# Another written-out order of all instructions on the five engines of an attention and MLP kernel

## The chip, the cores and the metric

The program runs on one core of one Trainium2 chip. A core has five engines with a queue each: TensorE (PE, matrix products; its weight loads are shown apart as PEld), VectorE (DVE), ScalarE (ACT), GpSimd (POOL) and SyncE (SP, which here issues every DMA). An engine works its queue strictly in order; between engines an instruction waits on semaphores. The metric is device time in microseconds of one execution, less is better. The kernel before took 799.24 us in the median of 3 runs (798.97 to 799.45).

## The reference

Three stages, all in float32, on 4 batches x 576 positions = 2304 tokens:

```
scores = scale * q @ k^T, causal;  a = softmax(scores);  local = a @ v
mem_out = (phi(q) @ M_prev) / (phi(q) . z_prev + 1e-6);  phi(x) = elu(x) + 1
x  = g * mem_out + (1 - g) * local          g = sigmoid(beta), one per head   8 heads x 64
x1 = (s * relu(x @ w_in)^2 + b) @ w_out     512 -> 2048 -> 512
h  = x1 @ w2_in                             512 -> 1024
y  = layernorm(h * softmax(h)) * g_ln @ w2_out      1024 -> 512
```

## The kernel before

Matrix products of the two MLPs split each float32 operand into a high and a low part and add three products (high x high, high x low, low x high), so every product is three `128x512` or `128x256` matmuls per 128 rows of depth. The larger ones are done by a Strassen-like scheme on 2x2 blocks: the block products are named X, Y, V and W.

The program has three stretches, by the trace:

- Attention, 0 to about 260 us. Sixteen pairs of heads, u = 0 to 15. For each pair: scores `s` (L730, L761), a row minimum by DVE into `mx` and the exponential by ACT (L713), transposes `pp` of the probabilities on PE (L787, and L799 for the last chunk into `ppu`), their copies `pt` by ACT (L791) and `ptl` by DVE (L800), then the values `po` (L819) and `pe` (L831), and the memory term (L835, L837) whose operand `mq` POOL weighs (L685) and DVE makes (L678). Beside it runs the first quarter of the first MLP as filler (`first_part`, `hidden`: L850 to L852, L913 to L915), and ACT and DVE decode and split the weights (`fetch`, `split_w`: L485 to L514).
- The rest of the first MLP, to about 600 us (`second_part`): ten rounds, each one block of tokens and six of the twelve remaining slices f of the hidden width. `y2_r_c` is the result of round r in output chunk c, `X_r_f` to `W_r_f` are the block products. Between PE steps stand the leaving operations: ACT copies (L1134, L1159), DVE additions (L1150 to L1166), the activation on ACT (L1126 to L1129) and its low part on DVE (L1130), and the addition of `y2` to `yT` on DVE (L1185). POOL builds the next round's block sums (L979 to L987) and the weights' sums (L530, L540).
- The second MLP, to the end (`mlp2`): nine pairs of token tiles; products a to d (L1273 to L1276), softmax and norm (`front`), transposes `zt` (L1322), copies `zh` (ACT, L1325) and `zl` (DVE, L1326), and the output product (L1331 to L1333).

What sets the order: nothing is left to a scheduler. `ORDER` is a table of runs `a+n` for each engine; a number is an instruction's place in the order in which the program text makes it, `a+n` means n of them from a. `state_order` chains each instruction to the one before it in that list, so the queue of each engine is exactly the list. `SLOTS` fixes which buffer each tile gets. The waits follow from the data and from the buffers.

```
for x, y in zip(seq, seq[1:]):
    tc.add_manual_dep(y, x.name, info, reason="order")
```

Of the kernel before, what the change touches and what calls it, by code (L numbers as in the profile page):

```python
# [26 lines left out]
0+22 34+4 22+6 46 38+2 48+8 28+2 47 62 30 66 31+2 63 33 40+3 64+2 43+3 67 56+2 71+2 58 73 59+2 68+3 114+2 74+6 116+4  # L27
84 80 85 81+2 86 83 87 102+4 61 88+4 106+4 92+3 96 95 122+4 110+4 97 101 98+3 147 120+2 126+6 148 132+2 149+2 146
151 195+2 155+6 134+2 161+2 197+2 163+2 136+8 183+2 144+2 185+3 165 152 166 153 167+2 154 203+4 199+2 207+4 169+4
177 188+4 173+3 178 176 179+2 438 181 228 182 192+2 201+2 211+4 236+6 215+2 194 217+10 229+4 439 227 233 242+2 234+2  # L30
244+2 284+2 276+2 286+2 278+4 288+4 246+4 440 250+4 264+4 254+3 258 257 268+8 259 263 260 309 261+2 282+2 308 310
292+16 317+2 357+4 319+4 361+2 441 311+6 345+4 442 323 327+2 324+3 329+2 365+8 331+4 443 390 444+3 335+5 349+8 344
340+4 389 391 363+2 373+4 398+6 377+12 447+3 392+3 430+6 450+8 395+3 408+2 483+5 404 410+2 405+3 488+7 412 418+4
527+5 417 413+4 532+7 436+2 495+6 580+5 475 585+6 476 591 458+12 422+6 470+2 428+2 472+2 539+4 547+2 543+2 549+6
477+2 480+3 479 624+5 505+2 501 507 502+2 508 504 629+2 474 631+2 509 633+3 510+5 572 669+7 573 676 545 555+3 546
558 515+10 592+4 636+2 596+2 677+4 574+3 559+6 525+2 565+4 644+2 638+2 646+2 640+2 648+4 569+2 721 577+3 598+4 722+3
602+5 725 571 611 607+4 726 681 727+6 682 642+2 652+4 689+2 733+4 691+2 737+2 693+2 612+10 656+8 622+2 664+2 766+3
683+3 666+2 769 668 770 695 686+2 696 688 697+2 741+8 771+2 699+5 773+2 778 708 704+4 709+4 749+4 739 775+3 779+4
740 786+4 818+2 790+2 713+4 753+2 717+2 755+6 719+2 761+2 838+6 820+2 844+2 822+2 783+3 826+5 792+4 765 831 796+4
832 763+2 806+6 833 805 800 834+4 863 846 801 847+3 802+3 886+12 865+2 824 867 825 864 923+12 850+8 812+2 858+2  # L40
814+2 860+2 816+2 915+2 871+6 968+2 881+3 868 884 869+2 970+10 877+4 917+2 935+2 919+2 937+6 885 1020+7 902 898+3
1027+3 960 1030+2 862 901 943+4 1065+11 961 1076 921+2 903+4 980+6 907+2 947+10 909+2 957+2 911+4 965+3 962 1109+4
986+4 1113+4 963+2 994 1012+2 1032+2 1014+2 1034+4 1016+2 1038+2 995 990+3 996+2 993 998 1117+2 1057 999 1119 959
1058 1120 1018 1040+4 1019 1077+4 1121+4 1081+2 1000+10 1044+8 1010+2 1052+4 1059+3 1129+4 1125+2 1154 1083 1062
1084 1063+2 1085+2 1155+5 1091 1133+4 1092+4 1087+3 1160+3 1090 1096 1163+4 1056 1239+3 1167 1242 1137+3 1127 1140
1128 1097+6 1174+2 1206+4 1176+2 1210+2 1178+2 1141+10 1103+6 1151+2 1168+3 1243 1153 1244+2 1171+3 1214+8 1180+3
1246 1183 1247+4 1184+3 1189+2 1187 1191+2 1251 1274+2 1188 1276+6 1193 1282+4 1252 1212 1222+2 1213 1224+2 1194+4
1336+12 1259+2 1303+4 1261+4 1226+2 1198+2 1228+6 1200+4 1234+2 1204+2 1236+2 1253+3 1371+4 1256 1265+3 1257 1268
1258 1307+2 1311+8 1375+3 1269 1273 1270+3 1378+3 1286+5 1348 1238 1381 1349 1382 1309+2 1356+4 1400+2 1360+2 1402+4
1291+12 1350 1319 1351 1320 1352 1321+2 1408+4 1362+4 1323+12 1412 1370 1413+2 1353+3 1383+4 1335 1366+4 1415+5 1445  # L50
1387 1420+8 1388+4 1428+2 1406 1430+2 1407 1462+4 1446 1432+8 1392+4 1440+2 1396+2 1442+2 1398+2 1466 1447 1453+4
1448+2 1467+4 1461 1471+3 1450 1474 1451+2 1475+3 1444 1491+12 1457+4 1479+4 1516+3 1478 1519+4 1483+4 1503+8 1487+2
1511+2 1489+2 1513+3 1528 1540+2 1529+5 1523 1534 1542 1535 1543 1536 1544+2 1524 1537 1546+2 1538+2 1548 1525
1549+6 1526 1555 1564 1556 1565+3 1527 1557 1568+3 1558+4 1571+5 1562 1576 1588 1577 1563 1589 1578 1590+2 1579 1592
1580 1593 1636 1624 1637+2 1625+2 1639 1627+3 1640+4 1630 1644 1631 1645 1632 1646 1633 1647 1634+2 1581+3 1594
1584+2 1648+7 1660 1655 1661+3 1656 1664+2 1657 1666 1595+2 1586+2 1597+3 1658+2 1667 1600+3 1612 1603 1613 1604+2
1614 1606+6 1668+4 1615+3 1720 1672+2 1618+6 1674+2 1726 1676+10 1727 1686+2 1721 1688 1696 1689 1697 1690 1698+3
1691+3 1701 1722 1694 1702 1695 1703+5 1728+3 1708 1723 1709+2 1738+4 1711+3 1742 1724 1714 1725 1715+3 1731 1743
1718+2 1744+4 1732+5 1768 1737 1748+2 1769+3 1756+3 1750+6 1759+4 1772 1763+2 1773 1765+2 1774 1780 1775 1781 1776
1767 1782 1777+2 1783+3 1779 1789+5 1795 1794 1786 1796 1804 1787 1813+2 1805 1815 1788 1806 1816+4 1822 1820 1823  # L60
1807 1824+2 1808 1826 1821 1809+4 1840 1797 1858 1798+2 1828 1800 1829+2 1827 1801 1831 1802 1832 1803 1859 1841
1867+3 1833+5 1843+2 1838 1845 1839 1846 1861+3 1847 1864+3 1860 1842 1849 1852 1848 1853+5 1879 1870 1850+2 1876
1871 1873+2 1872 1877 1880 1878 1875 1882 1906+2 1894 1915 1895 1908+2 1916 1900 1917+2 1896 1910 1901+2 1897+2 1911
1903 1899 1904 1919+2 1905 1888 1885 1881 1886 1891 1889 1883+2 1892+2 1890 1924 1948 1966+2 1925+2 1968 1936 1927
1949 1937 1928 1938 1969 1950 1939 1929 1951+3 1940+2 1970+2 1930 1912 1960+6 1978+2 1972 1980 1973 1981 1974+2 1987
1976 1988 1977 1989 1982+2 2020 1990+2 1931 1887 1921 2005+4 1992 2009+2 1933+2 1932 1913 1954 1922 1935 1914 1955
1957 1942 1923 1943 1958 1945+2 1944 1947 1959 1956 1996+2 2014+6 1998+4 2021+2 2026 2023 2027 2024 2028+2 2032+2
2030 2034 2025 2031 2035 2041 2036 2042+2 2037 2044+3 1984+2 2059+2 2050 2061 2051+5 2062+3 1993+2 2002 1995 1986
2011 2047 2012+2 2003 2038+2 2048 2040 2049 2065 2004 2066 2092+2 2104+4 2094 2113 2098 2108 2095 2114+3 2096 2117
2097 2118 2056 2068 2057+2 2067 2099 2109 2100+2 2122+2 2102+2 2124+2 2074 2069 2077 2071 2075 2072 2070 2073 2083  # L70
2076 2084 2080 2086 2081 2078+2 2146+3 2134 2149+2 2126 2135 2127 2151 2136 2164+2 2137+2 2166 2139 2158 2167 2159+4
2170+2 2176 2163 2172+3 2177 2175 2178+2 2168 2180+2 2169 2087 2082 2110 2089+3 2088 2128 2111 2085 2218 2185 2203+3
2186+2 2206 2219+2 2207+2 2188 2221+2 2189+2 2129 2112 2130 2140+2 2194 2212 2195+2 2224 2197+3 2225+2 2213 2227+2
2214 2223 2215 2230+2 2216+2 2229 2232 2119+3 2152 2142 2131 2143 2132+2 2155 2153 2144 2156+2 2145 2154 2239+2 2233
2257 2234 2241+2 2258 2235 2259+2 2243 2261+2 2244 2200 2182 2201+2 2209 2254 2183+2 2191 2236 2302+2 2290 2248 2291
2249 2304 2250+3 2292 2305 2253 2306 2293+3 2307 2192+2 2210 2245 2211 2255 2246 2256 2263+2 2237+2 2265 2247 2311+2
2296+3 2313 2299 2314+2 2300+2 2316 2266 2272 2275 2269+3 2273 2267 2276 2268 2278 2350 2338 2351+3 2339+5 2354+3
2274 2277 2344+5 2357+3 2349 2360+2 2287 2281 2279 2282 2284 2288 2283 2289 2285 2280 2286 2374+6 2308+2 2323 2310
2324 2326 2320 2325 2321 2335+2 2317+2 2337 2322 2332 2327 2319 2328+4 2333+2 2380 2386+6 2381+2 2392+3 2368 2362
2369 2395 2383 2396 2370 2384 2397 2385 2365 2455 2404 2371 2366+2 2405 2401 2363+2 2398 2446+2 2456 2399 2448  # L80
2457+2 2434+3 2402 2400 2372 2449 2403 2437 2406 2438 2373 2459 2407 2416 2410 2440 2411+2 2450 2408 2422 2417 2409
2419 2423 2413 2441+2 2424 2439 2418 2443 2428 2460 2444+2 2420 2451 2464+2 2452 2414+2 2466 2429 2467+2 2488 2469
2425 2453 2489 2421 2426 2431 2490 2500 2491+2 2501 2493 2502+2 2427 2506 2461 2504 2476+3 2507 2430 2454 2512
2508+2 2479+3 2505 2462 2470 2463 2432 2513+2 2433 2510 2473 2515 2511 2527 2471 2474 2518 2516 2519 2472 2528 2517
2520 2529 2560+2 2494 2530 2475 2545 2495 2521 2485 2546+2 2522 2496 2548 2523 2549 2531 2482+2 2532 2550 2562+2
2536+3 2484 2539+3 2564 2486 2554+3 2566 2497 2557+2 2487 2567 2498 2565 2568 2559 2569+2 2499 2572 2571 2573+2
2581+2 2575 2533 2524 2534+2 2583 2599 2576 2584 2577 2600+2 2585 2525 2551+2 2542 2553 2543 2586 2602+2 2590+2 2604
# [1317 lines left out]
```

## Time and profile before

| | |
|---|---|
| median of 3 runs | 799.24 us (798.97 to 799.45) |
| the profiled execution, as timed | 797.52 us |
| its span, first to last instruction | 795.7 us |
| PE busy | 784.8 us (99% of the span), 5298 matmuls |
| DVE, ACT, POOL busy | 598.6 (75%), 567.7 (71%), 155.6 us (20%) |
| granted TensorE clock over the span | 1.00 |
| chain that ended last | PE 82%, DVE 7%, ACT 4%, issue 3%, DMA 2% |

Line numbers as L831 are those of the kernel's text. An idle time in brackets at the end of a timeline row is the time in which the engine did nothing before that instruction, and behind the arrow what ended it. Matmuls overlap in the pipeline: their shown durations are longer than the distance between their starts, so throughput is read from starts.

### The profile page before, as it was taken

Reading aid. Unit: us, or ns where it says so; the run is one execution under the profiler, and the core shown is the slowest. Engines: PE = TensorE matmul, PEld = TensorE weight load, DVE = VectorE, ACT = ScalarE, POOL = GpSimd, SP = SyncE. Lnnn points to the kernel's source line nnn. Section 1 sums busy time; section 2 is a strip of 40 time slices with the busy share of each in tenths; the row PEclk is TensorE's granted clock in tenths of the full one; section 3 lists DMA queues with packets and bytes.
Section 4 is the critical chain, followed back from the end, with each engine's and each line's share of the span. In section 5 each row is a group of like instructions: output and inputs, shape, how many; then the busy total and the mean of one; then the engine's idle time right before and its main releaser. Section 6 shows DMA issues by size and latency. Waiting matters only on the chain.

```text
span 795.7 us, 14760 instructions
## 1 busy us (share of the span) xinstructions
PE 784.8 (99%) x5298; PEld 656.7 (83%) x5298; DVE 598.6 (75%) x1457; ACT 567.7 (71%) x1186; POOL 155.6 (20%) x166
## 2 busy tenths in 40 slices
PE   9999999999999999999999999999999999999998
PEld 7777777877776888889899888889987888888886
DVE  6999988877799888996557778566769665566751
ACT  7999988888897569987868776677746443445542
POOL 3121222122011324140120114000022212121200
PEclk9999999999999999999999999999999999999999
DMA  8463573464847558787687876576563001000001
GB/s 261 148 205 89 168 203 104 153 168 147 290 148 224 198 174 301 253 290 253 215 279 260 288 243 195 191 243 199 188 256 133 1 27 40 14 27 28 26 28 54
DMA packets 63277, 133.47 MB, mean 168 GB/s; under 512 B 9228, under 2 KB 19172, under 8 KB 63204
## 3 DMA queue, kind: packets, MB, share of 16 engines
q1 hardware_dynamic: 63204, 132.53, 50.5%
q8 instruction: 42, 0.69, 0.4%
q14 instruction: 31, 0.25, 0.1%
HBM read 90.97 MB, written 41.53 MB: 167 GB/s over the span
## 4 chain that ended last, share of the span: by engine, by line
PE 82%; DVE 7%; ACT 4%; issue 3%; DMA 2%; POOL 1%; SPq 0%; DVEq 0%; ACTq 0%; POOLq 0%
PE y L1181 5%; PE y L1179 5%; PE y L1180 5%; PE pp L787 5%; PE s L730 5%; PE V L1109 4%; PE X L1109 4%; PE o L1331 4%; PE o L1332 4%; PE o L1333 4%; PE po L819 4%; PE W L1109 3%; PE h L850 2%; PE h L851 2%; PE y L915 2%
## 5 line engine op out<-in xcount | busy, mean ns | idle before, releaser
L1180 PE MATMUL y<-g,w 128*128 128x512 f32 (+1 forms) x240 | 81.2, 370 | 0.0
L1179 PE MATMUL y<-g,w 128*128 128x512 f32 (+1 forms) x240 | 78.7, 371 | 0.9 <-DVE yT L1185 0.9
L1181 PE MATMUL y<-g,w 128*128 128x512 f32 (+1 forms) x240 | 78.9, 370 | 0.0
L713 ACT ACTIVATE pr<-pr,mx 128x128 f32<-128x128 f32 (+3 forms) x128 | 71.0, 558 | 3.8 <-DVE mx L746 3.4
L791 ACT ACTIVATE pt<-pp,omg 128x512 f32<-128x512 f32 (+3 forms) x128 | 62.8, 524 | 10.2 <-PE pp L787 9.1
L746 DVE CUSTOM_DVE_ANT_0 pr<-s,big 128x256 f32<-128x256 f32 (+3 forms) x128 | 59.1, 481 | 10.0 <-PE s L730 8.8
L1109 PE MATMUL X<-fhb,w 128*128 128x256 f32 x240 | 63.4, 285 | 0.7 <-ACT u L1134 0.5
L1109 PE MATMUL V<-fht,w 128*128 128x256 f32 x216 | 57.2, 286 | 0.8 <-ACT yo L917 0.3
L1332 PE MATMUL o<-w,zh 128*128 128x512 f32 x144 | 54.7, 393 | 0.0
L1331 PE MATMUL o<-w,zh 128*128 128x512 f32 x144 | 54.2, 392 | 0.0
L1333 PE MATMUL o<-w,zl 128*128 128x512 f32 x144 | 54.0, 393 | 0.0
L1130 DVE TENSOR_TENSOR g<-r,g 128x512 fp32r<-128x512 f32 (+1 forms) x60 | 40.1, 672 | 17.3 <-ACT r L1129 16.9
L1128 ACT ACTIVATE g<-r,b_sb,s_sb 128x512 fp32r<-128x512 f32 (+1 forms) x60 | 45.6, 767 | 9.7 <-PE y L1181 9.1
L1181 PEld LDWEIGHTS y<-g,w 128*128 128x128 f32 x240 | 44.8, 189 | 6.8 <-DVE g L1130 0.2
L1180 PEld LDWEIGHTS y<-g,w 128*128 128x128 f32 x240 | 44.7, 189 | 6.6
L787 PE MATMUL pp<-ident,pr 128*128 128x128 f32 x320 | 49.4, 276 | 0.2 <-DVE ptl L800 0.2
L1179 PEld LDWEIGHTS y<-g,w 128*128 128x128 f32 x240 | 43.6, 189 | 6.7 <-DVE yT L1185 1.1
L1126 ACT ACTIVATE r<-r 128x512 f32<-128x512 f32 (+1 forms) x60 | 34.7, 582 | 18.4 <-DVE r L1162 8.6
L624 POOL TENSOR_TENSOR q<-ph,zb 128x640 f32<-128x640 f32 x16 | 25.7, 1608 | 111.8 <-DVE ph L621 92.0
L787 PEld LDWEIGHTS pp<-ident,pr 128*128 128x128 f32 x320 | 37.8, 140 | 11.4 <-issue 2.2
L730 PE MATMUL s<-kq 64*128 64x128 f32 x640 | 46.5, 288 | 0.4 <-DVE sm L768 0.3
L1109 PEld LDWEIGHTS X<-fhb,w 128*128 128x128 f32 x240 | 44.3, 190 | 2.9 <-ACT r L1159 0.8
(233 smaller groups left out, 2371.1 us busy)
## 6 DMA issues: line engine op xcount, KB each, us to landing
raw<-in_moe_w_in_dram SPq DMA_DIRECT2D x24, 512.0 KB, 6.5
raw<-in_moe_w_out_dram SPq DMA_DIRECT2D x24, 512.0 KB, 4.1
wd<-wt SPq DMA_DIRECT2D x21, 512.0 KB, 4.7
w<-wd SPq DMA_DIRECT2D x21, 512.0 KB, 7.2
kq<-in_kq_dram SPq DMA_DIRECT2D x16, 608.0 KB, 5.7
RW<-rd SPq DMA_DIRECT2D x24, 288.0 KB, 4.8
q<-in_q_dram SPq DMA_DIRECT2D x16, 320.0 KB, 3.6
v<-in_v_dram SPq DMA_DIRECT2D x16, 320.0 KB, 6.0
```

Of the source, the lines that this page charges most:

```text
L713: mark[0] = nc.scalar.activation(pr, pr, AF.Exp, bias=mx, scale=-1.0, accum_out=sm).ins
L730: self.last = nc.tensor.matmul(ss[:, j, c0 + k * P:c0 + (k + 1) * P], x[:, S + i * P:S + (i + 1) * P], x[:, k * P:(k + 1) * P], start=True ...
L746: nc.vector.tensor_tensor_reduce(pr, ss[:, j, at[i]:at[i] + n], big[:, CF * P - i * P:CF * P - i * P + n], -scale, FMAX, ALU.add, ALU.min, mx)
L787: nc.tensor.transpose(pp[:, e * n + c * P:e * n + (c + 1) * P], pr[:, c * P:(c + 1) * P], ident)
L791: nc.scalar.activation(p["pt", i // 2][:, j, 0:i + 1, i % 2, :], pp[:, e * n:(e + 1) * n].rearrange("p (c t) -> p c t", t=P), AF.Copy, sca ...
L1109: nc.tensor.matmul(o, wc[a], b[:, i, 0:m], start=(i == 0 and z == 0 and not more), stop=(i == KH - 1 and z == 2), skip_group_check=True)
L1179: nc.tensor.matmul(o, wc[0], gh, start=(f == fs[0]), stop=False)
L1180: nc.tensor.matmul(o, wc[1], gh, start=False, stop=False)
L1181: nc.tensor.matmul(o, wc[0], gl, start=False, stop=(f == fs[-1]))
L1331: nc.tensor.matmul(oo, zh, w[:, 0], start=(f == 0), stop=False)
L1332: nc.tensor.matmul(oo, zh, w[:, 1], start=False, stop=False)
L1333: nc.tensor.matmul(oo, zl, w[:, 0], start=False, stop=(f == NF2 - 1))
```

## The change

Only the numbers in `ORDER` change. The instructions, their count on every engine, the buffers in `SLOTS` and all text below are the same; each of the five queues is another permutation of the same list. The new lists come from a search that judged an order by the mean of four replays with drawn lengths and landings. On PE 558 of 4546 instructions keep their place, on ACT 225 of 1005, on DVE 235 of 1243, on POOL 67 of 166, on SP 68 of 366; most move by a few places.

```
 ORDER = {
     "PE": """
-0+22 34+4 22+6 46 38+2 48+8 28+2 47 62 30 66 31+2 63 33 40+3 64+2 43+3 67 56+2 71+2 58 73 59+2 68+3 114+2 74+6 116+4
...
     "SP": """
-17+2 20 32 29 28 21 19 24 27 26 33 25 22 30 23 37 31 41 34 36 42 54 45 39 35 49 40 60 47 44 43 46 38 48 50 53 55 52
+17+2 28 20 19 45 21 23 32 24 33 22 25 46 31 37 41 26 36 30 34+2 39 42 49 40 38 29 54 43+2 47+2 27 50 60 53 55 52
```

Three places, as the built programs list them (operation, output <- inputs, shape; "x2": two alike in a row).

First, DVE at the end of the attention, between the product that closes pair 14 (`po14`) and the copy `ptl` of pair 15's last transposed chunk (`ppu15`), for which the matmuls `pe15` wait. Before:

```order
L838 TENSOR_TENSOR xb3_3005<-po14_3444,RW14_3413 128x512
L678 SCALAR_TENSOR_TENSOR mq15_3481<-kq15_3142,mq15_3481 128x640
L491 TENSOR_TENSOR wa12_2110<-wa12_2110,raw12_2108 128x512
L488 TENSOR_SCALAR raw14_3782<-wa14_3784 128x512
L490 SCALAR_TENSOR_TENSOR raw14_3782<-raw14_3782 128x512
L880 TENSOR_TENSOR xl3_3714<-xb3_3005,xh3_3713 128x320
L509 TENSOR_TENSOR w11_1917<-wa11_1911,w11_1917 128x512
L880 TENSOR_TENSOR xl3_3714<-xb3_3005,xh3_3713 128x320 x2
L491 TENSOR_TENSOR wa14_3784<-wa14_3784,raw14_3782 128x512
L509 TENSOR_TENSOR w13_2260<-wa13_2254,w13_2260 128x512
L800 COPY ptl_137<-ppu15_3619 64x128
```

The same stretch now:

```order
L838 TENSOR_TENSOR xb3_3005<-po14_3444,RW14_3413 128x512
L509 TENSOR_TENSOR w10_1792<-wa10_1786,w10_1792 128x512
L678 SCALAR_TENSOR_TENSOR mq15_3481<-kq15_3142,mq15_3481 128x640
L488 TENSOR_SCALAR raw18_4185<-wa18_4187 128x512
L509 TENSOR_TENSOR w12_2116<-wa12_2110,w12_2116 128x512
L490 SCALAR_TENSOR_TENSOR raw18_4185<-raw18_4185 128x512
L800 COPY ptl_137<-ppu15_3619 64x128
```

Ten instructions stood between the two ends and were passed; now there are five. The three additions L880 stand behind the copy.

Second, DVE in the second round of `second_part` (r = 1), before the addition L1185 that frees the PSUM bank of `y2_0_1`, for which the first matmul of `y2_1_1` waits. Before:

```order
L1150 TENSOR_TENSOR u1_8_4703<-Y_1_8_4698,u1_8_4703 128x256
L1153 TENSOR_TENSOR u1_8_4703<-V_1_8_4699,u1_8_4703 128x256
L1156 TENSOR_TENSOR r2_1_9_4705<-W_1_8_4700,u1_8_4703 128x256
L509 TENSOR_TENSOR wt0_5187<-ss12_5072,wt0_5187 128x512
L1185 TENSOR_TENSOR yT_4102<-y2_0_1_4114,yT_4102 128x512
```

Now:

```order
L1130 TENSOR_TENSOR g2_1_5_4495<-r2_1_5_4498,g2_1_5_4495 128x512
L486 TENSOR_SCALAR wa33_5065<-wa33_5065 128x512
L1156 TENSOR_TENSOR r2_1_7_4619<-W_1_6_4614,u1_6_4617 128x256
L488 TENSOR_SCALAR raw33_5063<-wa33_5065 128x512
L1130 TENSOR_TENSOR g2_1_4_4494<-r2_1_4_4497,g2_1_4_4494 128x512
L1185 TENSOR_TENSOR yT_4102<-y2_0_1_4114,yT_4102 128x512
```

The addition moved ahead of all work on f = 8: in front of it stand results of f = 4 and f = 6, whose products PE has done earlier.

Third, PE in the third round (r = 2), between the last matmul of `X_2_8` and the first of `X_3_4`, which takes over the same PSUM bank once ACT has copied `X_2_8` out (L1159). The last rows before:

```order
L1179 MATMUL y2_2_2_4855<-g2_2_5_4862,w9_1595 128x512
L1180 MATMUL y2_2_0_4853<-g2_2_4_4861,w8_1456 128x512
L1181 MATMUL y2_2_0_4853<-g2_2_4_4861,w8_1456 128x512
L1179 MATMUL y2_2_1_4854<-g2_2_4_4861,w8_1456 128x512
L1179 MATMUL y2_2_0_4853<-g2_2_5_4862,w9_1595 128x512
L1109 MATMUL V_3_4_5226<-fht3_3_5197,w15_3874 128x256
L1109 MATMUL V_3_4_5226<-flt3_3_5198,w15_3874 128x256
L1109 MATMUL X_3_4_5224<-fhb11_3_5191,w14_3804 128x256
```

Now:

```order
L1109 MATMUL X_2_8_5080<-fhb21_2_4816,w22_4241 128x256
L1109 MATMUL V_2_8_5082<-fht4_2_4814,w23_4324 128x256
L1181 MATMUL y2_2_3_4856<-g2_2_4_4861,w8_1456 128x512
L1179 MATMUL y2_2_3_4856<-g2_2_5_4862,w9_1595 128x512
L1180 MATMUL y2_2_3_4856<-g2_2_5_4862,w9_1595 128x512
L1181 MATMUL y2_2_3_4856<-g2_2_5_4862,w9_1595 128x512
L1179 MATMUL y2_2_0_4853<-g2_2_5_4862,w9_1595 128x512
L1109 MATMUL V_3_4_5226<-fht3_3_5197,w15_3874 128x256
L1109 MATMUL X_3_4_5224<-fhb11_3_5191,w14_3804 128x256
```

Between the two stood ten matmuls of `128x512` and two of `128x256` (five of the ten are not shown); now five and two.

## Rows read from the trace of the kernel before

**Rows 1.** The page, busy us of each engine, share of the span, instructions

```profile
PE 784.8 (99%) x5298; PEld 656.7 (83%) x5298; DVE 598.6 (75%) x1457; ACT 567.7 (71%) x1186; POOL 155.6 (20%) x166
```

**Rows 2.** Stretches: from:to, length, then busy us (x instructions) by engine

```profile
0.00:20.00 20.00, 18.85 (x163) 14.44 (x163) 12.83 (x57) 14.43 (x40) 6.92 (x20) 1.00 0.82 262
780.00:800.00 20.00, 12.02 (x53) 9.58 (x52) 1.38 (x2) 2.88 (x5) 0.00 (x0) 0.93 0.15 53
```

**Rows 3.** Waits of PE: instruction <- releaser: us, times, longest

```profile
PE warm L379 <- DVE mhalf L1240: 1.1, 1, 1.1
PE pe L831 <- DVE ptl L800: 1.0, 1, 1.0
PE y L1179 <- DVE yT L1185: 0.9, 1, 0.9
PE zt L1322 <- DVE var L1309: 0.6, 1, 0.6
PE X L1109 <- ACT u L1134: 0.5, 1, 0.5
PE zt L1322 <- DVE sm L1302: 0.4, 1, 0.4
...
```

**Rows 4.** Groups of PE instructions by shape: busy us, mean ns

```profile
L1180 PE MATMUL y<-g,w 128*128 128x512 f32 x192 | 68.7, 392 | 0.0
L850 PE MATMUL h<-xh,w 128*128 128x512 f32 x64 | 27.2, 435 | 0.0
L851 PE MATMUL h<-xl,w 128*128 128x512 f32 x64 | 25.7, 410 | 0.0
```

**Rows 5.** Timeline of PE at 432 us: start, us, instruction, count

```profile
432.41 0.28 PE L1109 MATMUL W<-fht,wh 128*128 128x256 f32 x1
432.53 0.40 PE L1109 MATMUL V<-fht,w 128*128 128x256 f32 x2
...
433.13 0.86 PE L1180 MATMUL y<-g,w 128*128 128x512 f32 x3
433.82 0.40 PE L1181 MATMUL y<-g,w 128*128 128x512 f32 x1
```

**Rows 6.** Timeline from 253 us: DVE, POOL and PE before the copy ptl

```profile
253.01 0.69 DVE L509 TENSOR_TENSOR w<-wa,w 128x512 fp32r<-128x512 f32 x1
...
254.66 1.95 POOL L685 TENSOR_TENSOR mq<-mq,RW 128x640 f32<-128x640 f32 x1 [11.42 <-DVE xl L880]
...
255.12 2.04 DVE L509 TENSOR_TENSOR w<-wa,w 128x512 fp32r<-128x512 f32 x1
...
257.19 0.29 DVE L800 COPY ptl<-ppu 64x128 f32<-64x128 f32 x1
...
257.54 0.69 PE L831 MATMUL pe<-ptl,v 128*64 128x64 f32 x16 [1.03 <-DVE ptl L800]
```

**Rows 7.** Timeline from 342 us: the same engines before y of round 1

```profile
342.84 1.31 POOL L980 TENSOR_TENSOR xr<-xr 128x512 f32<-128x512 f32 x1
...
342.91 1.78 DVE L509 TENSOR_TENSOR wt<-ss,wt 128x512 fp32r<-128x512 f32 x1
...
344.62 1.27 DVE L1185 TENSOR_TENSOR yT<-y,yT 128x512 f32<-128x512 f32 x2
...
345.35 0.50 PE L1179 MATMUL y<-g,w 128*128 128x512 f32 x1 [0.85 <-DVE yT L1185]
```

**Rows 8.** Timeline from 294 us: copies out of PSUM, and PE behind them

```profile
294.12 0.39 ACT L917 ACTIVATE yo<-y 128x256 f32<-128x256 f32 x1 [0.21 <-PE y L915]
...
298.08 0.39 ACT L917 ACTIVATE yo<-y 128x256 f32<-128x256 f32 x1 [0.63 <-DMA yd<-yo]
...
298.52 0.39 PE L1109 MATMUL V<-fht,w 128*128 128x256 f32 x1 [0.28 <-ACT yo L917]
```

**Rows 9.** Timeline from 377 us: the copy by ACT before the first matmul of X_3_4

```profile
378.39 0.36 ACT L1159 ACTIVATE r<-X 128x256 f32<-128x256 f32 x1
...
378.80 0.39 PE L1109 MATMUL X<-fhb,w 128*128 128x256 f32 x1
```

440 rows, old and new, of the table ORDER are left out of this document.

## The prediction

> **What bounds the kernel now.** I read the page first: PE is busy for 784.8 of 795.7 us [rows 1]; no other engine comes near. Then the stretches: the last one shown holds 12.02 us of PE work [rows 2], so the last matmul ends about 3.7 us before the span does, and the final copy and store fill that. What PE idles beyond that stands in its waits. That view has 15 rows of one wait each: 1.1 us before the first matmul, then 1.0, 0.9, 0.6, 0.5 and 0.4, and nine of 0.2 or 0.3 with 2.5 us together [rows 3]. So 5.9 us inside the program are waits on another engine's result, and 5.9 + 1.1 + 3.7 = 10.7 is nearly all of the 10.9 us that PE does not work. An order can win the 5.9, not the start or the end.
>
> There is a second, hidden loss. In the attention the same `128x512` matmul of the filler takes 435 ns (L850) to 410 (L851) where in the later stretch it takes 392 (L1180) [rows 4]. Six lines of 64 matmuls are of this kind, so between 6 x 64 x 18 ns = 6.9 us and 6 x 64 x 43 ns = 16.5 us go there, about 12 in the middle; PE changes between kinds of work there, and a follower starts late.
>
> For cover I need the price of PE work by starts: a `128x256` matmul starts 0.12 us after the one before, a `128x512` one (433.82 - 433.13) / 3 = 0.23 us [rows 5].
>
> **The change part by part.** Nothing is added or removed, so each term is a wait that goes, shrinks or grows. For each I ask how much PE work stands in the order between the last matmul that the awaited result needs (with what is queued ahead of it) and the matmul that waits; call it the cover.
>
> *The copy before `pe15` (1.0 us).* DVE's L509 there took 2.04 us, its neighbour of the same form 0.69 [rows 6]: POOL's L685 ran from 254.66 to 256.61, and L509 ended 0.55 us behind it. The copy (0.29) was queued behind, and PE waited 1.03. Between `po14` and the copy DVE now passes five instructions, not ten; with `po14`'s own addition that is six, at the 0.69 us of an undisturbed L509 each 4.1 us, plus 1.35 if POOL's operation falls on an L509 again: 5.5. PE has 6.9 us of its own work from the end of `po14` to `pe15` (before: 6.4), and about 1.1 us from the chunk's transpose, which the copy with 0.29 us fits into. I take -1.0, ends 0 and -1.0.
>
> *The addition before `y2_1_1` (0.9 us).* Again an L509 beside POOL: 1.78 us, 342.91 to 344.69, with L980 until 344.15; L1185 starts 344.62 and PE idles 0.85 [rows 7]. Now the addition stands ahead of all work on f = 8, with no L509 in the six rows, and its cover grows from 2.25 to 4.5 us. I take -0.9, ends 0 and -0.9.
>
> *The pair of waits at 297 and 298 us (0.5 and 0.3).* The first goes: `X_0_4` now has seven `128x256` matmuls, 0.84 us, behind the last matmul that its copy needs, where it had none, and the copy takes 0.38. What is late next is the second. `yo4_3` takes over the buffer of `yo4_2`, and may be written only when that one's store has landed: copy at 294.12, landed at 298.0, next copy at 298.08, `V_0_4` at 298.52 [rows 8], 4.4 us in all. PE's own work from `y4_2` to `V_0_4` is 3.48 us before and 3.60 now. So the stall of 0.8 moves to V and shrinks by 0.12; I take -0.1, ends 0 and -0.5.
>
> *Six smaller ones.* Before `zt` the cover of the three waits of 0.6, 0.4 and 0.3 grows by 0.23, 1.0 and over 5 us: -0.2, -0.4, -0.3. Three waits of 0.3 (at 234, 411 and 440 us) get 0.7 us of cover or more: -0.9. Together -1.8, ends 0 and -2.2.
>
> *What gets worse.* `X_3_4` waits for ACT's copy L1159 of `X_2_8`. The copy itself is 0.36 us, but ACT came to it only at 378.39, and the matmul started at 378.80 [rows 9]. Cover before: ten and two matmuls, 2.5 us; now five and two, 1.4. If ACT is as late as it was, PE waits 1.1 us more; if ACT is in step, the 0.36 hide and it costs nothing. ACT has nearly the same five operations ahead. Two more places lose 0.5 (`W_0_8` at 316) and 0.4 us (`X_7_10` at 494) of cover. Ends 0 and +2.0; I take the middle, +1.0.
>
> *Changes of kind on PE in the attention.* Counted in the two lists, 373 before and 360 now, 3.5% fewer. Of the hidden 12 us that is -0.4, ends 0 and -0.6.
>
> *Waits not there before.* Over both lists I counted the cover of every wait of PE for ACT, DVE or POOL: 686 and 688. Under 1.0 us there are 57 before and 47 now, under 2.0 us 324 and 294. If waits go with the close ones, 5.9 x 47/57 = 4.9 us would remain, a gain of only 1.0; the named terms give -1.0 - 0.9 - 0.1 - 1.8 + 1.0 - 0.4 = -3.2. The two disagree because a new order has its own unlucky places, which this trace cannot show. I add +0.7 for them, between none and the +2.2 that would bring the two together.
>
> *SP and the weights.* The reloads of weights and block forms keep their distance: the shortest PE work between what releases a reload of a form (L951) and its matmul is 4.1 us before and 5.0 now. At the start the second pair's keys are fifth in SP's list, not eighth. No wait of PE before ends on a landing directly, so I put both at nothing; cover gone there would cost a landing, which was 3.5 us for the store above.
>
> Sum: -3.2 + 0.7 = -2.5 us. On the profiled execution, 797.52 (1.8 around a span of 795.7), that is 795.0. The median of the runs is 1.7 above that execution, so the forecast is 799.24 - 2.5 = **796.7 us**.
>
> **The rivals.** *The waits come back elsewhere (no change).* For it: half the listed gains are single waits of 0.2 to 0.4 us, and 294 places with under 2 us of cover remain, on engines that are 71 and 75% busy [rows 1]. Against it: the close places got fewer in every class. If the whole 3.2 returns, 799.2; with the fewer close ones, 798.2.
>
> *DVE meets POOL at worse places (slower).* The two dearest waits were not of the order alone: each had a DVE addition that took 1.1 to 1.35 us longer beside a POOL operation [rows 6, 7]. DVE's list moved against POOL's nearly unmoved one, so the meetings fall elsewhere. In `second_part`, where POOL builds the block sums of the next round, an L1130 or L509 ahead of an L1153 or L1156 holds up a product on PE. Each such meeting with a cover under 1.2 us costs up to 1.2. It turns slower at four uncovered new ones (4 x 1.2 - 2.5 = +2.3): 801.5 us. For it: W and V products with a cover of 1.1 us are still there. Against: two in 795 us were uncovered before.
> The Trainium skill ("SBUF — State Buffer", section "SBUF: two separate sides") says that VectorE and GpSimd share a port pair as an exclusive lock for a whole instruction, and that a VectorE operation with two SBUF inputs blocks fully against a GpSimd one that reads SBUF. The trace agrees at both places, where the addition ended 0.55 us after POOL's did. By that rule a meeting could cost as much as the whole POOL operation, 1.95 us for L685, and four would give 804.5.
>
> *Everything listed is won and nothing new comes.* All 5.9 us and 0.6 of the changes of kind: 792.7. Little speaks for it, since the store at 298 us stays.
>
> **How the numbers follow.** A measurement of this kernel can tell 0.2%, 1.6 us, from no change; 797.6 and 800.8 are the bounds. The forecast, 794 to 797.6, has 0.52, with 0.05 for the case that all is won below it: faster 0.57. Waits that come back, 797.6 to 800.8, have 0.24; meetings, above 800.8, 0.19. The range leaves out about one in ten on either side: 793.3 to 801.3.
>
> **What would show it.** Right: no row for `pe` L831 and `y` L1179 in PE's waits, or a few tenths; L509 of about 0.7 us ahead of the copy `ptl`; a wait of V for `yo` at about 298 us of 0.6 to 0.9, and none of X there; the waits of PE after the first at 3 to 4 us together; L850 below 435 ns. Wrong: a sum of waits near 5.9, or L1153, L1156 and L1130 stretched above 1 us in front of a waiting W or V; then the slower case holds. If PE's busy time changes by more than 2 us without its waits, my split into waits and changes of kind is at fault.

## The result and the profile after

The changed kernel takes 787.77 us in the median (785.34 to 791.80, six runs) against 799.11 (796.76 to 799.97, six runs) of the kernel before on the same chip: ratio 0.987 (0.984 to 0.990), 11.3 us less. The forecast was 2.5 less, and the time lies below its range. Two later sets of runs gave 786.09 against 797.82 and 786.55 against 797.65.

The page of the profiled execution after (790.62 us as timed, 788.8 span) answers to [rows 1]:

```profile
PE 779.0 (99%) x5298; PEld 657.1 (83%) x5298; DVE 593.4 (75%) x1457; ACT 568.2 (72%) x1186; POOL 155.7 (20%) x166
```

PE works on the same 5298 matmuls and is busy 5.8 us less. The whole list of its waits (instruction, releaser, us, times, longest), against the 15 of [rows 3]:

```profile
PE pp L787 <- ACT pt L791: 2.5, 1, 2.5
PE warm L379 <- DVE mhalf L1240: 1.1, 1, 1.1
PE V L1109 <- ACT yo L917: 1.0, 1, 1.0
PE zt L1322 <- DVE z L1311: 0.7, 2, 0.4
PE pp L787 <- DVE xb L839: 0.4, 1, 0.4
PE s L761 <- DVE mx L746: 0.3, 1, 0.3
```

`pe` and `y` are gone, and X too. The 2.5 and the 1.0 do not come in every execution: a later profile of the same kernel (783.6 us span) has neither. Its page, and its waits after the first matmul's 1.1:

```profile
PE 777.3 (99%) x5298; PEld 655.8 (84%) x5298; DVE 591.9 (76%) x1457; ACT 567.8 (72%) x1186; POOL 155.7 (20%) x166
```

```profile
PE zt L1322 <- DVE z L1311: 0.7, 2, 0.4
PE pp L787 <- DVE xb L839: 0.3, 1, 0.3
PE s L761 <- DVE mx L746: 0.3, 1, 0.3
```

I compare this one with before, since neither is disturbed. The span shrinks by 795.7 - 783.6 = 12.1 us: 7.5 of it is shown as less PE busy time, and only 4.6 as less idle time. To place it, I priced each matmul by the commonest distance from its start to the next, by form (0.227 us for `128x512`, 0.120 for `128x256`, and so on; the same sum for either kernel), and summed what the starts took beyond that. That loss falls from 33.0 to 29.2 us in the attention, from 8.8 to 2.3 in the rest of the first MLP, from 3.1 to 1.5 in the second. Its level depends on how finely forms are told apart, the differences hardly do.

The copy that answers to [rows 6]; timeline of the profile after (start, us, engine, instruction):

```profile
252.96 0.68 DVE L509 TENSOR_TENSOR w<-wa,w 128x512 fp32r<-128x512 f32 x1
...
254.63 0.69 DVE L509 TENSOR_TENSOR w<-wa,w 128x512 fp32r<-128x512 f32 x1
...
256.48 0.29 DVE L800 COPY ptl<-ppu 64x128 f32<-64x128 f32 x1 [0.57 <-PE ppu L799]
...
257.52 0.40 PE L831 MATMUL pe<-ptl,v 128*64 128x64 f32 x8
```

DVE now waits for the transpose, and PE does not wait for the copy. The copies that answer to [rows 8], first in the profile after:

```profile
293.25 0.75 ACT L917 ACTIVATE yo<-y 128x256 f32<-128x256 f32 x2 [1.26 <-PE y L915]
...
297.70 0.38 ACT L917 ACTIVATE yo<-y 128x256 f32<-128x256 f32 x1 [1.23 <-DMA yd<-yo]
...
298.13 0.39 PE L1109 MATMUL V<-fht,w 128*128 128x256 f32 x1 [1.01 <-ACT yo L917]
```

The same copy in the later execution, where the store landed earlier:

```profile
292.40 0.38 ACT L917 ACTIVATE yo<-y 128x256 f32<-128x256 f32 x1
```

### The profile page after: what moved, and what is told of

Same layout as the page of the kernel before. It is cut to its first block, busy times and chain, and to the rows that moved or that the text cites. A ratio compares the mean times of both kernels' runs of the same rounds, so it can differ in the third digit from the quotient of the medians.

```text
span 788.8 us, 14752 instructions
## 1 busy us (share of the span) xinstructions
PE 779.0 (99%) x5298; PEld 657.1 (83%) x5298; DVE 593.4 (75%) x1457; ACT 568.2 (72%) x1186; POOL 155.7 (20%) x166
## 4 chain that ended last, share of the span: by engine, by line
PE 93%; DMA 3%; DVE 2%; issue 1%; SPq 0%; POOL 0%; ACT 0%; ACTq 0%; DVEq 0%
PE y L1179 6%; PE y L1181 6%; PE y L1180 6%; PE pp L787 5%; PE V L1109 5%; PE X L1109 5%; PE s L730 5%; PE po L819 5%; PE W L1109 4%; PE o L1333 4%; PE o L1331 4%; PE o L1332 4%; PE Y L1109 2%; PE y L913 2%; PE zt L1322 2%; PE y L915 2%
## 5 line engine op out<-in xcount | busy, mean ns | idle before, releaser
L1181 PE MATMUL y<-g,w 128*128 128x512 f32 (+1 forms) x240 | 81.3, 370 | 0.0
L1179 PE MATMUL y<-g,w 128*128 128x512 f32 (+1 forms) x240 | 80.2, 370 | 0.0
L1180 PE MATMUL y<-g,w 128*128 128x512 f32 (+1 forms) x240 | 80.1, 370 | 0.0
L713 ACT ACTIVATE pr<-pr,mx 128x256 f32<-128x256 f32 (+3 forms) x128 | 70.9, 556 | 2.0 <-DVE mx L746 1.6
L791 ACT ACTIVATE pt<-pp,omg 128x256 f32<-128x256 f32 (+3 forms) x128 | 62.8, 524 | 11.3 <-PE pp L787 7.4
L746 DVE CUSTOM_DVE_ANT_0 pr<-s,big 128x128 f32<-128x128 f32 (+3 forms) x128 | 58.8, 481 | 10.3 <-PE s L730 9.8
L787 PE MATMUL pp<-ident,pr 128*128 128x128 f32 x320 | 51.6, 278 | 2.9 <-ACT pt L791 2.5
L1332 PE MATMUL o<-w,zh 128*128 128x512 f32 x144 | 54.1, 393 | 0.0
L1331 PE MATMUL o<-w,zh 128*128 128x512 f32 x144 | 52.5, 390 | 0.0
L1325 ACT ACTIVATE zh<-zt 128x512 fp32r<-128x512 f32 x36 | 21.0, 594 | 42.4 <-PE o L1332 29.4
```

Source lines behind the costliest of these rows:

```text
L713: mark[0] = nc.scalar.activation(pr, pr, AF.Exp, bias=mx, scale=-1.0, accum_out=sm).ins
L746: nc.vector.tensor_tensor_reduce(pr, ss[:, j, at[i]:at[i] + n], big[:, CF * P - i * P:CF * P - i * P + n], -scale, FMAX, ALU.add, ALU.min, mx)
L787: nc.tensor.transpose(pp[:, e * n + c * P:e * n + (c + 1) * P], pr[:, c * P:(c + 1) * P], ident)
L791: nc.scalar.activation(p["pt", i // 2][:, j, 0:i + 1, i % 2, :], pp[:, e * n:(e + 1) * n].rearrange("p (c t) -> p c t", t=P), AF.Copy, sca ...
L1179: nc.tensor.matmul(o, wc[0], gh, start=(f == fs[0]), stop=False)
L1180: nc.tensor.matmul(o, wc[1], gh, start=False, stop=False)
```

## The experiments

My theory, formed on the two traces: the gain is waits of PE, and most of a wait is in no row. In the trace before, 49 matmuls start within 0.08 us of the end of the operation that releases them, 28 of them after 261 us; in the trace after it is 13, with 3 after 261 us and 10 in the attention (the expectations of the two halves below have these two the other way round). Those 28 started 6.5 us late together, against the distance of their forms, and the next two starts behind each another 2.6. I call this the start delay. Rivals: only the shown waits count; or the gain is in PE's own order, its changes of kind. Medians stand beside the kernel before on the same chip (797.82, 797.63 and 797.65 us for the three sets). In traces of rewritten lists the line numbers are 4 or 5 lower.

### The two halves, and the whole

```
e1_att_before:  each queue: entries before 261 us from the old list, then the new list
e2_att_after:   each queue: entries before 261 us from the new list, then the old list
```

> The changed kernel once more, beside its parts on the same chip. Every theory: 0.987 of the kernel before, 785 to 788 us where TensorE is not held up at 210 us. If the 2.5 us wait of pp at 213 us belongs to the order itself, it stands in this profile too, with a granted clock below 1.00 behind it; if it was a stray late landing of that one execution, PE shows no wait over 1.2 us.

> The order before for the first 261 us (attention and the first quarter of the MLP), the changed order for the rest. Theory 1 (the gain is waits of PE, hidden ones too: start delays behind a releaser were 6.5 us plus 2.6 us in the next two starts over 28 waits after 261 us before, 10 waits after the change): this part alone gives -7 us, 792 us. Rival (only the waits that the profile shows count): the shown waits after 261 us that go are some 3 us, 796 us. Second rival (the gain is in the attention): 799 us.

> The changed order for the first 261 us, the order before for the rest. Theory 1: the 21 close starts of the attention become 3, -4 us, 795 us, and less by up to 4 where the 2.5 us wait at 213 us is there; with the other half it adds up to the whole, -11. Rival (only the shown waits): pe L831 1.0 and little more, 798 us. Second rival (the gain is in the attention): 788 us. If the two halves do not add up, each needs the other.

The whole again: 786.09 us, -11.7 (ratio 0.985, 0.983 to 0.988), without the wait at 213 us. The new second part alone: 792.81, -5.0 (0.993, 0.991 to 0.996). The new attention alone: 792.70, -5.1 (0.993, 0.991 to 0.995). Together 10.1 of 11.7: the halves nearly add up, and neither rival that puts all in one place holds, nor the one that counts only the shown waits (796 and 798 us). My sizes were off by 2 and 1. The first half-kernel pays at the seam between the two lists, the second at 212 us; one row of either, timeline of PE:

```profile
266.88 0.51 PE L846 MATMUL h<-xh,w 128*128 128x512 f32 x1 [1.38 <-ACT xh L875]
```

```profile
211.91 0.55 PE L782 MATMUL pp<-ident,pr 128*128 128x128 f32 x3 [1.46 <-ACT pt L786]
```

### Two moves on DVE alone

```
 DVE, kernel before
-L509 w13 / L800 ptl        -L509 wt0 / L1185 y2_0_1
+L800 ptl / L509 w13        +L1185 y2_0_1 / L509 wt0
```

> The kernel before with two moves on DVE alone: the copy L800 of ppu15 goes ahead of the L509 of w13 that stood in front of it, the addition L1185 of y2_0_1 ahead of the L509 of wt0. Theory (a wait of PE costs its whole start delay, also what the shown end of the matmul ahead covers): the rows pe L831 (1.0) and y L1179 (0.9) go, the matmuls start 1.2 and 1.0 us earlier, -2.2 us. Rival 1 (given back at the next uncovered place): 0 to -0.5, with new rows in PE's waits within 20 us. Rival 2 (the prediction's reading, the shown 1.03 and 0.85): -1.9; the times cannot part it from the theory, the starts in the trace can.

797.02 us beside 797.63, ratio 0.9994 (0.998 to 1.0006): the time cannot tell it from nothing, and it leaves out the -2.2 that the theory forecast and the -1.9 of rival 2. PE's list is that of before, so the same matmul can be followed in both traces. At `pe15` the new trace stands 1.16 us better than just ahead of it, at `y2_1_1` 0.98 us, about the full start delays of 1.21 and 1.01 and not the shown 1.03 and 0.85. So far the theory is right. But by the same starts 0.36 comes back at V (298.7 us), where the store of `yo` landed later, 0.54 at Y, 6 us behind the second move, and 0.66 at 558 us; the first and the last I cannot tie to the moves. That leaves 0.6 us, as the medians have it. The row of Y (timeline):

```profile
349.55 2.37 DVE L969 TENSOR_TENSOR flt<-xr,fht 128x512 fp32r<-128x512 f32 x2
...
350.14 0.39 PE L1105 MATMUL Y<-fht,w 128*128 128x256 f32 x1 [0.33 <-ACT fht L968]
```

Y needs the block sums, and that chain over POOL, DVE and ACT was not sped up. So the wait removed at 257 us was kept for 41 us, and of the one at 345 half was given back within 6: by the time rival 1, by the starts rival 1 in part. (This execution also lost 1.1 us at 218 us, ahead of either move.)

### POOL's operations cut short

```
-nc.gpsimd.tensor_tensor(b12, b22, b12, ALU.subtract)
+nc.gpsimd.tensor_tensor(b12[:, 0:1, 0:64], b22[:, 0:1, 0:64], b12[:, 0:1, 0:64], ALU.subtract)
 (the same for L540, L685, L979, L982, L987)
```

> The kernel before, with the in-place POOL operations L540, L685, L979, L980, L982 and L987 cut to 64 columns (most of their arithmetic is left out; the count, the order and all waits stay). Theory that DVE's meetings with POOL made the waits of before: of the 9.1 us of start delay after 261 us about 4.3 stood behind a DVE operation that had been stretched beside POOL; pe L831 and y L1179 vanish, L509 is 0.7 in front of both, -3 to -4 us, 794. Rival (the waits come from the distance in the order, with or without POOL): 0 to -1 us, 797 to 798, and the two rows stay.

> The changed kernel with the same cut of POOL's in-place operations to 64 columns (most of their arithmetic is left out). The cut took 5.1 us from the kernel before. Theory (the new order's results come early enough that a DVE operation stretched beside POOL no longer reaches PE): -0 to -1.5 us, 785 to 787, so the distance between the two orders without these meetings is 6 to 7 us: 5 of the 11.7 were meetings that reached PE. Rival (the meetings cost the new order as much as the old): -4 to -5, 781 to 782, the distance stays 11.

On the kernel before: 792.47 us, -5.2 (0.994, 0.993 to 0.996), more than forecast, and the rows of `pe` and `y` are gone. On the changed one: 785.65 beside 786.55, -0.9. So with the cut the two orders stand 6.8 us apart instead of 11.1, and up to 4.3 us were meetings that reached PE in the old order and not in the new. This is an upper end, for two reasons. The profile of the changed kernel with the cut has a wait behind a store's landing that the undisturbed one has not, so that up to 2.3 may stand behind its -0.9:

```profile
PE V L1109 <- ACT yo L917: 1.4, 1, 1.4
```

And the cut also brings POOL's own results earlier. None of the 15 rows of [rows 3] names POOL, but the run does not part the two. DVE operations beside POOL that took over 0.15 us longer than the lower quarter of their form lost some 28 us before and 8 with the cut; the changed kernel still has some 20 of them, at less cost. In front of `pe15` with the cut, against the 2.04 of [rows 6]:

```profile
253.27 0.79 POOL L685 TENSOR_TENSOR mq<-mq,RW 128x64 f32<-128x64 f32 x1 [12.47 <-DVE xl L880]
...
253.79 0.81 DVE L509 TENSOR_TENSOR w<-wa,w 128x512 fp32r<-128x512 f32 x1
254.63 0.29 DVE L800 COPY ptl<-ppu 64x128 f32<-64x128 f32 x1
```

The prediction weighed a lock that one of the two engines holds for a whole instruction, by the Trainium skill ("SBUF — State Buffer", section "SBUF: two separate sides"). The trace agrees: with POOL's operation at 0.79 us as at 1.95, L509 ends 0.54 or 0.55 us behind it.

### Every result earlier, PE's list untouched

```
-nc.vector.tensor_tensor(a, a, lf, ALU.add)
+nc.vector.tensor_tensor(a[:, 0:64], a[:, 0:64], lf[:, 0:64], ALU.add)
 (the same for L486, L488, L490, L1185 on DVE and L1126, L1127, L1129 on ACT, with the cut of POOL)
```

> The kernel before, with POOL cut as in the pool run and also the in-place work of DVE and ACT cut to 64 columns: the decoding L486, L488, L490, L491, the addition L1185, and the activations L1126, L1127, L1129 (most of their arithmetic is left out; order, count and waits stay). Every result that PE waits for is then there earlier, and TensorE's list is untouched. Theory (what the change won is waits, most of them hidden under shown matmul ends): 8 to 10 us go, 788 to 790, without a change on PE. Rival (what it won lies in TensorE's own order, fewer and cheaper changes of kind): only the shown waits go, -4 to -5, 793.

> The changed kernel with the same cuts. Theory: few waits are left to remove, -1 to -3, 783 to 785; the distance to the same cuts of the kernel before shrinks from 11.7 us to 3 or 4, of which 2.5 are changes of kind in the attention (transitions cost 32.4 us there before and 28.4 after, by starts, and waits explain 1.5 of the 4.0). Rival (TensorE's own order): the distance stays at 9 or more.

789.18 us, -8.5 (0.990, 0.988 to 0.992), and 786.14 on the changed kernel: none of its time goes, where 1 to 3 us were forecast. Its profile has the wait of V of 1.4 again and one of `pp` of 0.7 at 211 us, neither of them in the undisturbed one, and they may hide what the cut won. The distance shrinks from 11.7 to 3.0; without these two waits, and the 0.6 that V waits in the old order's run, it would be about 4.4. Either way it parts the theories: TensorE's order of before, unaltered, comes within 3 to 4.4 us of the new one once results come early, and not 9 or more. Page of the old order with the cut:

```profile
PE 779.6 (99%) x5298; PEld 657.1 (83%) x5298; DVE 503.4 (64%) x1457; ACT 511.1 (65%) x1186; POOL 112.7 (14%) x166
```

PE's busy time fell by 5.2 of the 8.3 us of span, with no matmul changed: busy time held waits. One of them, timeline of the kernel before:

```profile
439.20 0.28 PE L1109 MATMUL Y<-flt,w 128*128 128x256 f32 x1
439.34 0.41 DVE L1156 TENSOR_TENSOR r<-W,u 128x256 f32<-128x256 f32 x1
...
439.81 0.39 PE L1109 MATMUL W<-fhb,w 128*128 128x256 f32 x1 [0.33 <-DVE r L1156]
...
440.03 0.28 PE L1109 MATMUL W<-flb,w 128*128 128x256 f32 x1
```

and the same matmuls with the cut:

```profile
433.20 0.28 PE L1109 MATMUL Y<-flt,w 128*128 128x256 f32 x1
...
433.31 0.28 PE L1109 MATMUL W<-fhb,w 128*128 128x256 f32 x1
433.43 0.28 PE L1109 MATMUL W<-flb,w 128*128 128x256 f32 x1
```

From Y to W 0.61 us against 0.11, and from W to the next 0.22 against 0.12: 0.60 us lost where the row shows 0.33, for the shown end of Y (0.28) covers 0.17 and the start behind the wait is slow. Behind a matmul of this form a wait below 0.17 us shows no idle at all.

What is left between the two orders: the old one keeps 1.4 us of waits before `zt` and 0.5 before X in this run, the new one 0.8 and none. By starts this is 1.4 us in the second MLP and 1.0 in the rest of the first, although V waits longer there in the new order; some 1.2 us of the latter is in no row, and I have not traced it. In the attention the loss by starts is 29.6 against 29.0 us, or 28.3 without the wait of `pp`: that leaves 0.6 to 1.3 us at most for changes of kind.

### Three tries to better the changed kernel

```
e3_raw8_first:  SP  -rd12 store / raw8 load        +raw8 load / rd12 store
e7_xb2_late:    e3 and the store of xb2 behind the load of raw10
e8_v_later:     e7 and, on PE, V_0_4 nine matmuls back; L1166 and L1134 of that round earlier
```

> The changed kernel with one instruction of SP moved: the load of raw8 (a piece of w_out) goes ahead of the store rd12, behind which it stood while SP waited 4.8 us for rt12. Theory: the load is issued about 5 us earlier, ACT's L485 at 212 us no longer waits 3.5 us for it, PE's pp no longer 2.5 us, and the granted clock stays at 1.00 there: 785 to 786 us in every run, where the changed kernel spreads from 785 to 792. Rival: the landing is late because the DMA engines are full at 205 us, and an earlier issue lands as late: the wait stays, and the time and its spread are those of the changed kernel.

> The changed kernel with two moves on SP: the load of raw8 ahead of the store rd12, and the 1152 KB store of xb2 (issued at 199 us) behind the load of raw10, some 10 us later. Theory (the lone move of raw8 failed since the DMA engines were full with xb2 and the rows RW12 came late): no wait over 0.5 us between 205 and 220 us, 785.5 in the median. Rival (a late landing there is chance and moves to another transfer): as the changed kernel, 786 to 788.

> The run before with a third edit: on PE the six matmuls of V_0_4 at 293 us go nine matmuls further back (1.1 us) with the rest of that round's block products re-lined to keep their distances, one addition (L1166) and one copy (L1134) moved one to two places forward to suit. Theory: V no longer waits for the copy yo4_3 behind the store of yo4_2 (1.0 us in three of the traces, none in one), 785 us. Rival: other products of the round become late, -0 or a loss of up to 1 us.

> The changed kernel again, for comparison on the same chip: 786 to 788 us by every theory.

None is better. The load alone: 787.93 beside 786.09, so the rival held; another load and `mq` were late (timeline of ACT and PE):

```profile
215.18 0.67 ACT L481 ACTIVATE wa<-raw 128x512 f32<-128x512 f32 x1 [2.02 <-DMA raw<-in_moe_w_out_dram]
...
216.05 0.34 PE L831 MATMUL pe<-mq,Mb 128*64 128x64 f32 x4 [1.09 <-POOL mq L681]
```

With the store moved as well: 786.72 beside 786.55, no wait between 205 and 220 us in its trace, and another in its place at 100 us:

```profile
100.06 0.94 PE L726 MATMUL s<-kq 64*128 64x128 f32 x12 [0.99 <-DMA kq<-in_kq_dram]
```

With V later: 788.20. V no longer waits, but ACT does, and what is queued behind its copy is late on PE; the rival held, at 1.5 us:

```profile
293.61 0.39 ACT L913 ACTIVATE yo<-y 128x256 f32<-128x256 f32 x1 [1.48 <-DMA yd<-yo]
```

```profile
295.70 0.39 PE L1105 MATMUL X<-fhb,w 128*128 128x256 f32 x1 [0.68 <-ACT r L1155]
...
301.73 0.96 PE L1175 MATMUL y<-g,w 128*128 128x512 f32 x3 [1.17 <-ACT g L1124]
```

Whether a late landing in the changed kernel can be ordered away, rather than shifted, stays open.

## Why the prediction was wrong

The sign was right, and so was the view that an order wins or loses waits of PE; how they were priced and found was not. The step that failed is the first: "An order can win the 5.9, not the start or the end." It took PE's 784.8 busy us as work that no order shortens, apart from a term of 0.4 us. The runs show 5.2 us of waits inside that busy time by the cut of results alone, and 7.5 us less of it in the undisturbed profile after. The text had named the sign itself: busy time that changes by more than 2 us without its waits.

A rule of the Trainium skill speaks to that very step, and I did not weigh it: "Perfetto Trace Analysis", section "Identifying the Most-Contended Engine", says that matmul busy time does not tell how near a kernel is to its limit, since matmuls are pipelined. The trace agrees on the rule (99% in both, at 795.7 and 783.6 us) and differs on the direction: the page has pipelined instructions look smaller, here a `128x512` matmul is shown for 392 ns [rows 4] and the next one starts 0.23 us after it [rows 5].

Step by step, forecast first and then what the traces and runs showed:

- **The copy before `pe15`**, -1.0: right, -1.2 by starts.
- **The addition before `y2_1_1`**, -0.9: right, -1.0; alone, 0.54 of it comes back.
- **The pair at 297 and 298**, -0.1: X's wait went as said. V's grew to 1.0 in one execution and was absent in two: a landing sets it, 3.7 us behind the copy in the one, at most 2.4 in the later profile. Of all eight traces with this part of the new order, five show the wait, at 1.0 to 1.4. By starts that makes +0.1 or -1.1; I take the middle, about -0.6.
- **Six smaller ones**, -1.8: before `zt` 1.3 became 0.7. The other three went, but were worth 0.5 to 0.6 each by starts and not 0.3, so -0.6 and -1.7: -2.3 in all.
- **What gets worse**, +1.0: 0, for none of the three waits is in the trace after.
- **Changes of kind**, -0.4: too small by up to 1 us (0.6 to 1.3 at most; I take -1.0), and its sign in the profile, L850 below 435 ns, was wrong: it shows 441 in both profiles of the new order. That mean says nothing here.
- **Waits not there before**, +0.7: 0.6 to 0.7, all in the attention. The term was a middle that named no place, so that it came out is luck.

With these sizes the named steps give -1.2 - 1.0 - 0.6 - 2.3 - 1.0 + 0.7 = -5.4. The remaining 6 us of the 11.3 are, in the main, waits that the prediction could not name, because they had no row: 28 close starts after 261 us, where the view listed 10 waits. That they are waits rests on the cut of every result, which took 8.5 us with PE's list as it was, more than all the 5.9 us listed. The argument that was to allow for others failed too: covers under 1 us went from 57 to 47, but actual waits from 49 to 13. The count of short covers did not scale with the waits, since what made them wait was a late engine, for up to 4.3 us of it a DVE operation beside POOL. The rival of worse meetings had the right mechanism and the wrong sign: they cost PE less in the new order.

## What to carry to other kernels

On a bound engine whose shown instruction is longer than the distance between its starts, price waits by starts: compare each start with the spacing of its form, and do not take busy time as a floor. An experiment that brings every awaited result forward without touching the bound engine's list tells how much of its busy time, at least, is waiting. A wait removed alone may be kept only up to the next uncovered chain, as at Y here, so judge an order whole.

## What was not expected of the hardware

In the profile after, TensorE stood idle from 210.85 to 213.39 us, and its clock fell. Windows (from:to, length, PE, PEld, DVE, ACT, POOL busy, granted clock, DMA share, GB/s):

```profile
212.00:213.00 1.00, 0.00 (x0) 0.00 (x0) 0.25 (x1) 0.94 (x3) 0.00 (x0) 1.00 0.80 281
213.00:214.00 1.00, 0.61 (x3) 0.50 (x3) 0.97 (x4) 1.00 (x4) 0.00 (x0) 0.52 0.09 33
...
215.00:216.00 1.00, 1.00 (x14) 1.00 (x12) 1.00 (x1) 0.00 (x0) 0.77 (x1) 0.50 0.00 0
216.00:217.00 1.00, 1.00 (x18) 0.88 (x17) 1.00 (x3) 0.63 (x1) 0.00 (x0) 0.78 0.00 0
```

0.50 is 1.2 GHz, the lower of its two levels. By these shares it held from about 213.0 us, while TensorE still stood idle, to about 216.4. PE's list is the same in the later, undisturbed profile, so each matmul can be followed: between 210 and 217 us the profile after falls 4.05 us behind, 1.5 more than the shown wait of 2.55. That execution took 790.62 us, where the next set of runs had 786.09 in the median. One more of the six runs, 791.80 us, has a granted clock below 1.00 (0.996, here 0.998) and no trace, so this may have come twice. In the half-kernel with the idle time of 1.46 us at the same place the clock stayed at 1.00. The cause was a load: ACT, timeline of the profile after.

```profile
212.06 0.66 ACT L485 ACTIVATE wa<-raw 128x512 f32<-128x512 f32 x1 [3.46 <-DMA raw<-in_moe_w_out_dram]
...
213.39 0.90 PE L787 MATMUL pp<-ident,pr 128*128 128x128 f32 x3 [2.55 <-ACT pt L791]
```
